# Swapped weights in the attention products, transposes after them, and unread operations behind the last store

## The chip, the cores and the metric

One core of a Trainium2 chip runs the program. TensorE (PE) multiplies matrices, VectorE (DVE) and ScalarE (ACT) work elementwise, GpSimd (POOL) prepares masks, SyncE (SP) issues most DMAs. Each engine executes its own instructions in order, and engines wait for each other by semaphores. The metric is the device time of one execution in microseconds (us); lower is better.

## The reference

Attention over 8 batches x 8 heads x 576 positions x 64, whose first four heads see a causal window of 32 positions and whose last four see every fourth position of a window of 128; then a feed-forward network of width 2048 on the 4608 x 512 result.

```python
scores = scale * np.matmul(q, k.transpose(0, 1, 3, 2))
mask_plain = (rel >= 0) & (rel < window)
mask_dil = (rel >= 0) & (rel < window * dilation) & (rel % dilation == 0)
scores = np.where(masks[None, :, :, :], scores, -1000000000.0)
attn = np.exp(scores - np.max(scores, axis=-1, keepdims=True))
attn = attn / (np.sum(attn, axis=-1, keepdims=True) + 1e-09)
out = np.matmul(attn, v)
# heads side by side, then
h = x @ w_in
g = 0.5 * h * (1.0 + erf(h * inv_sqrt2))
return g @ w_out
```

## The kernel before

The 4608 positions are worked on in nine chunks of 512. Chunk 0 to 7 are the first 512 positions of each batch, chunk 8 holds the last 64 of all batches. Within a chunk the heads go in four pairs, p0 and p1 plain, p2 and p3 with every fourth position. Chunk 8's p2 and p3 are called wide: their windows have 96 keys, the others' 64.

The feed-forward network splits every fp32 number into a rounded part and a rest, so that each product is three matmuls of 128 x 128 weights and 512 columns. For each chunk `ffn_h` makes h in 16 blocks f of 12 matmuls (line 537), `ffn_gelu` applies the gelu on ScalarE and splits the result into g on ScalarE and VectorE, and `ffn_o` makes the output in 16 x 12 matmuls (line 560). A unit below is 12 of these matmuls, so a chunk has 32 units. The order in a chunk is: eight blocks of h, their o, the other eight blocks of h, their o; in the last part the four output blocks d finish one after the other, at units 26, 28, 30 and 32, each with a copy (line 98 or 100) and a store.

The attention of chunk c + 1 is laid into the network of chunk c. `add(c, at, rank, gen)` puts a step at a unit of that chunk, and the steps are emitted as soon as the loop has passed their unit; among equal units a lower rank goes first. Scores (line 296) stand at units 2 and 4, the exponentials from 8.5, the normalisation and `turn` (which lays keys onto partitions by 32 x 32 transposes on VectorE, lines 418 and 423) from 10.5. `av` multiplies attention weights and v: p0 and p1 at unit 24.75, p2 and p3 at 26.75; `xout` then copies the result from PSUM to x on ScalarE (line 98) and subtracts to get the rest on VectorE (line 524). The network's next chunk reads x from unit 32 on. Chunks 0 and 1 are laid out differently, by an order written out by hand, and are not touched by the change.

PSUM is one tile `ps` of eight banks. Banks 0 to 3 hold o, and the scores in between; banks 4 and 5 hold h, and banks 4 to 7 the results of `av`. A quarter of the columns of all four banks belongs to each pair.

In `av` (line 493) v is the weights: 64 keys on the rows, the 64 columns of one head's v. The turned attention weights of 32 queries stream, so a product writes 64 partitions (the head's dimensions) x 32 columns (queries). A pair has 32 such products, which the profile records as 64, since an fp32 product is two. The result has the dimensions on partitions, as the network needs it.

Buffers come from pools: `wpool` (tag "w") holds the network's weights and, by turns, loaded q, k and v; `work` (tag "sm", 7 buffers) holds softmax tiles and turned weights; `xg` holds x, g and scratch.

Of the kernel before, what the change touches and what calls it, by code (L numbers as in the profile page):

```python
# [7 lines left out]
F32 = mybir.dt.float32  # L8
F32R = mybir.dt.float32r
BF16 = mybir.dt.bfloat16  # L10
U32 = mybir.dt.uint32
U16 = mybir.dt.uint16
AF = mybir.ActivationFunctionType
ALU = mybir.AluOpType
AX = mybir.AxisListType

B, H, S, D = 8, 8, 576, 64
WIN, DIL = 32, 4
DM, DFF = H * D, 2048
P = 128  # L20
N = 512
# [6 lines left out]
KB, NU = 32, 4  # L28
# [39 lines left out]
def at_once(gen):  # L68

    e = next(gen)  # L70
    try:
        while True:
            e = gen.send(e[0])
    except StopIteration:
        pass
# [3 lines left out]
def attn_ffn(ctx: ExitStack, tc: tile.TileContext, qk, qk_lp, qk_ld, v, v_ld, w, outT):  # L79
    nc = tc.nc  # L80
    const = ctx.enter_context(tc.tile_pool(name="const", bufs=1))
    wpool = ctx.enter_context(tc.tile_pool(name="wpool", bufs=NF + NW_SPARE))
    xg = ctx.enter_context(tc.tile_pool(name="xg", bufs=12))
    work = ctx.enter_context(tc.tile_pool(name="work", bufs=2))
# [3 lines left out]
    ps = psum.tile([P, 8, 512], F32, name="ps")  # L88
# [179 lines left out]
    def slot(s, u):  # L268
        return u if s.plain or s.rest or s.c < 2 else (u - 1) % NU
# [202 lines left out]
                            to = to[:, (2 * r + a) * KB:(2 * r + a + 1) * KB]  # L472
                        nc.tensor.matmul(to, s.v[rows, a, r, h * D:(h + 1) * D], t, start=True, stop=True)  # L473

    def av(s, px, u0=0):

        yield "p"
        s.px = px
        if s.wide:
            for u in range(u0, u0 + 2):  # L480
                for m in range(3):
                    for r in range(4):
                        rows = slice(32 * r, 32 * r + 32)
                        for h in range(2):
                            nc.tensor.matmul(px(r)[h * D:(h + 1) * D, u * KB:(u + 1) * KB], s.v[rows, u, m, h * D:(h + 1) * D],  # L485
                                             s.t[h][rows, 3 * u + m], start=m == 0, stop=m == 2)
            return
        for u in range(NU):
            for j in range(2):
                for r in (j, 2 + j):  # L490
                    rows = slice(r // 2 * 64, r // 2 * 64 + 64)
                    for h in range(2):
                        nc.tensor.matmul(px(r)[h * D:(h + 1) * D, u * KB:(u + 1) * KB], s.v[rows, u, j, h * D:(h + 1) * D],  # L493
                                         s.t[rows, h * NU + slot(s, u), j], start=True, stop=True)

    def px_four(p, bank):

        return (lambda r: ps[:, bank + r, p * P:(p + 1) * P]), ps[:, bank:bank + 4, p * P:(p + 1) * P]

    def xout(s, px):  # L500
        e = yield "ad" if s.c < 2 else "a"
        s.x = xg.tile([P, 2, N], F32R, tag="xg", name="x")
        if s.wide:
            put = []
            for b in range(2):
                src = px[:, :, b * 64:(b + 1) * 64].rearrange("p r (g i) -> p r g i", g=4)
                dst = [s.x[:, t].rearrange("p (r b i g) -> p r b g i", r=4, b=2, g=4)[:, :, b] for t in range(2)]
                put.append((src, dst))
        elif s.c < 2:

            px = ps[:, s.bank + 1] if s.wide_v else ps[:, s.bank:s.bank + 2, s.p % 2 * 256:s.p % 2 * 256 + 256]
            to = [s.x[:, t] if s.wide_v else s.x[:, t].rearrange("p (k n) -> p k n", k=2) for t in range(2)]
            if s.wide_v and s.plain:
                px = px.rearrange("p (b d i) -> p b d i", d=DIL, i=8)
                to = [y.rearrange("p (d b i) -> p b d i", d=DIL, i=8) for y in to]
            put = [(px, to)]
        else:
            put = [(px, [s.x[:, t].rearrange("p (r i) -> p r i" if s.plain or s.rest else "p (i r) -> p r i", r=4)
                         for t in range(2)])]
        for y, (h, l) in put:  # L520
            copy(e, h, y)
        yield "d"
        for y, (h, l) in put:
            nc.vector.tensor_sub(l, y, h)  # L524
# [44 lines left out]
    def store(c, d, parts=1):  # L569
        for i in range(parts):  # L570
            n = N // parts
            cols = slice(i * n, (i + 1) * n)
            e = yield "ad" if i % 2 == 0 else "d"
            o = work.tile([P, N], F32, tag="go", name="o_sb", bufs=3)
            copy(e, o[:, cols], ps[:, d, cols])
            yield "q"
            (nc.scalar if parts > 1 and e == "a" else nc.sync).dma_start(
                outT[d * P:(d + 1) * P, c * N + i * n:c * N + (i + 1) * n], o[:, cols])
# [5 lines left out]
    jobs = {}  # L584
# [9 lines left out]
    for f in range(NF):  # L594
# [4 lines left out]
        for i, cols in enumerate(parts(f)):  # L599
            k = f"{f}.{i}" if f < HALVED else f"{f}"  # L600
# [7 lines left out]
    for c in range(3):  # L608
        for p in range(NPAIR):
            s, k = xs[c][p], f"{c}.{p}"  # L610
            jobs["qk" + k] = load(s)
            if c == 2:
                continue
            if p % 2 == 0:
                jobs["v" + k] = load_v(s)
            if c == 0:
                jobs["scores" + k] = scores(s, (4, 0, 2, 6)[p])
                jobs["av" + k] = av_wide(s)
                for i in range(2):
                    jobs[f"half{k}.{i}"] = turn_half(s, i)  # L620
            elif p % 2 == 0:
                jobs["scores" + k] = one("p", [scores(xs[c][p + i], 6) for i in range(2)])
                jobs["av" + k] = one("p", [av_early(xs[c][p + i]) for i in range(2)])
            if c == 0 or p % 2 == 0:
                jobs["low" + k] = lowest_two(s, xs[c][p + 1]) if c else lowest(s)
                jobs["sums" + k] = inverse(s)
            jobs["exp" + k] = softmax(s)
            if s.subtract:
                jobs["sub" + k] = subtract(s)
                jobs["sum" + k] = sum_up(s)  # L630
            jobs["norm" + k] = norm(s)
            jobs["turn" + k] = turn_pe(s)
            jobs["x" + k] = xout(s, None)
    for d in range(NC):
        jobs[f"store0.{d}"] = store(0, d)

# [1 line left out]
    for i in range(BURN):  # L638
        rows = slice(32 * (i % 4), 32 * (i % 4) + 32)
        nc.tensor.matmul(ps[rows, 7, 0:2 * KB], ones[rows, 0:KB], ones[rows], start=True, stop=True)  # L640
    begun, ended, wants = set(), set(), {}
    for token in SCHEDULE.split():
        name, _, times = token.partition("*")
        name, _, e = name.partition(":")
        times = int(times or 1)
        if name == "fill":
            bank = 7
# [22 lines left out]
    def add(c, at, rank, gen):  # L670
        steps.append((2 * NF * c + at, rank, len(steps), gen))
# [5 lines left out]
                at_once(f)  # L677
        return gen()

    A_SC, A_E, A_N, A_X, A_QK, A_V = (2, 4), 8.5, 10.5, (24.75, 26.75), 26.5, 3  # L680
    for n in range(2, NCH):
        c = n - 1
        s = xs[n]
        late = n == LAST
        for p in range(NPAIR):
            wide = late and p >= 2
            bank = 4 + 2 * (p - 2) if wide else p // 2 * 2
            if c > 1:
                add(c, (3.25 + .25 * (p % 2)) if wide else A_QK - 32 + .25 * p, 0, load(s[p]))
            add(c, A_SC[p // 2] if not wide else 8.25, 1, scores(s[p], bank))  # L690
            add(c, A_SC[p // 2] + .5 + p % 2 if not wide else 8.5 + (p - 2), 2, lowest(s[p]))
            add(c, A_E + p + (.5 if wide else 0), 3, softmax(s[p]))
            add(c, A_N + p * 1.5 + (.5 if wide else 0), 4, inverse(s[p]))
            add(c, A_N + p * 1.5 + (.5 if wide else 0), 4, norm(s[p]))
            add(c, A_N + p * 1.5 + (.5 if wide else 0), 5, turn(s[p]))
            px = px_four(p, 4)
            at = A_X[p // 2] + (1.75 * (p - 2) if wide else 0)
            for u in (range(0, NU, 2) if wide else [0]):
                add(c, at + .75 * u, 6, av(s[p], px[0], u))
            add(c, at + (1.75 if wide else .25 + p % 2 / 2), 7, xout(s[p], px[1]))  # L700
        add(c, A_V, 0, load_v(s[0]))
        if late:
            add(c, 9, 0, load_v_wide(s[2]))
            add(c, 9.25, 0, load_v_wide(s[3]))
        else:
            add(c, A_V + .25, 0, load_v(s[2]))
    steps.sort(key=lambda t: t[:3])
    at = 0
# [8 lines left out]
    for c in range(1, NCH):  # L717
        gs = {}
        base = 2 * NF * c
        for f in range(half):  # L720
            at_once(ffn_h(c, f, gs))
            upto(base + f + 1)
        for f in range(half):
            for d in range(NC):
                ffn_o(d, f, gs)
                upto(base + half + f + (d + 1) / 4)
        for f in range(half, NF):
            at_once(ffn_h(c, f, gs))
            upto(base + half + f + 1)
        for d in range(NC):  # L730
            for f in range(half, NF):
                ffn_o(d, f, gs)
                upto(base + 3 * half + 2 * d + (f - half + 1) / 4)
            at_once(store(c, d, 2 if c == LAST and d == NC - 1 else 1))


# [99 lines left out]
```

## Time and profile before

| | us |
|---|---|
| median of two runs | 886.18 (885.46 to 886.9) |
| the profiled execution | 885.41 |
| its span | 883.6 |
| PE busy | 871.6 |
| DVE busy | 352.1 |
| ACT busy | 380.6 |
| POOL busy | 9.5 |

The span runs from the first instruction of the profile to the end of the last, transfers included; the execution's own time holds a little around it. A row of a group reads: line, engine, operation, what is written and read with shapes, count, then busy time in us, mean duration of one in ns, and the idle time of the engine ahead of it with what ended it. A row of the timeline reads: start, length in us, engine, line, operation, count. Matmuls overlap in these records, so the time that a block of them takes is read from its start to the start of the next block. PEld is the loading of weights, which runs beside the matmuls.

### The profile page before, as it was taken

To read this page: it belongs to the slowest core of one execution; us is meant where nothing else is said; L and a number is where in the kernel's file an instruction comes from. 1 tells how busy PE (TensorE), PEld (TensorE's weight loads), DVE (VectorE), ACT (ScalarE), POOL (GpSimd) and SP (SyncE) were. 2 spreads that over 40 slices of the span, in tenths; PEclk is the share of its full clock that TensorE was granted. 3 is DMA by queue.
4 is the path that set the end of the run, shared out by engine and by line. 5 is a ranking of instruction groups with operands and counts; after the bars stand their busy time and mean duration, and the time that the engine had idled before them with its cause. 6 is when DMAs were issued, how large, how long until landed. Compare 5 with 4: busy or idle time off the path is not lost.

```text
span 883.6 us, 18852 instructions
## 1 busy us (share of the span) xinstructions
PE 871.6 (99%) x8304; PEld 719.4 (81%) x8304; DVE 352.1 (40%) x597; ACT 380.6 (43%) x1016; POOL 9.5 (1%) x46
## 2 busy tenths in 40 slices
PE   7999999999999999999999999999999999999998
PEld 5888888888888888888888888888888888878886
DVE  8899934621462126321552146213622163212020
ACT  7798535442363227232544235423733272314040
POOL 1000020000000000000000000000000000000000
PEclk9999999999999999999999999999999999999999
DMA  9997431003300330024000510033002410010001
GB/s 363 416 420 281 143 101 46 1 1 134 107 0 1 121 120 1 1 92 148 3 1 1 172 69 0 1 133 108 1 1 85 167 73 1 13 38 1 0 1 48
DMA packets 16930, 75.39 MB, mean 85 GB/s; under 512 B 1872, under 2 KB 2128, under 8 KB 12496
## 3 DMA queue, kind: packets, MB, share of 16 engines
q1 hardware_dynamic: 16704, 74.06, 22.5%
q8 instruction: 65, 1.06, 0.5%
q14 instruction: 17, 0.14, 0.1%
q10 hardware_dynamic: 144, 0.13, 0.0%
HBM read 64.75 MB, written 9.44 MB: 84 GB/s over the span
## 4 chain that ended last, share of the span: by engine, by line
PE 97%; DMA 2%; SPq 0%; issue 0%; DVE 0%; ACT 0%; ACTq 0%; DVEq 0%
PE ps L560 45%; PE ps L537 45%; PE ps L493 3%; PE ps L296 3%; DMA raw_w<-w 2%; PE ps L485 1%; PE ps L473 0%; PE ps L431 0%; PE ps L454 0%; SPq L245 0%; PE ps L282 0%; ACT zeroed L98 0%; SPq L166 0%; DVE spare L190 0%; DVE sm L405 0%
## 5 line engine op out<-in xcount | busy, mean ns | idle before, releaser
L560 PE MATMUL ps<-g,weight 128*128 128x512 f32 x1728 | 401.7, 390 | 0.0
L537 PE MATMUL ps<-x,weight 128*128 128x512 f32 x1728 | 401.3, 390 | 0.0
L537 PEld LDWEIGHTS ps<-x,weight 128*128 128x128 f32 x1728 | 322.9, 188 | 67.9
L560 PEld LDWEIGHTS ps<-g,weight 128*128 128x128 f32 x1728 | 322.9, 188 | 67.2
L549 DVE TENSOR_TENSOR g<-gf,g 128x512 fp32r<-128x512 f32 x144 | 99.7, 693 | 382.6 <-ACT g L98 382.5
L544 ACT ACTIVATE gf<-ps 128x512 f32<-128x512 f32 x144 | 86.1, 598 | 311.1 <-PE ps L537 311.1
L98 ACT CAST g<-gf 128x512 fp32r<-128x512 f32 x143 | 88.8, 621 | 4.5
L380 ACT ACTIVATE sm<-sm,st 128x64 f32<-128x64 f32 (+1 forms) x224 | 74.9, 337 | 0.1
L98 ACT COPY o_sb<-ps 128x512 f32<-128x512 f32 (+1 forms) x34 | 19.7, 582 | 108.4 <-PE ps L560 103.8
L524 DVE TENSOR_TENSOR x<-ps,x 128x512 fp32r<-128x512 f32 (+1 forms) x38 | 30.2, 805 | 86.8 <-ACT x L98 86.8
L98 ACT CAST x<-ps 128x512 fp32r<-128x512 f32 (+1 forms) x37 | 27.0, 749 | 58.9 <-PE ps L493 40.6
L423 DVE STREAM_TRANSPOSE turned<-sm 32x256 f32<-32x256 f32 x104 | 45.4, 436 | 2.0
L380 ACT ACTIVATION_READ_ACCUMULATOR sm<-sm,st 128x1 f32 x224 | 42.1, 188 | 0.0
L296 PEld LDWEIGHTS ps<-raw_qk 64*32 64x32 f32 x2304 | 26.0, 110 | 9.3 <-issue 5.4
L296 PE MATMUL ps<-raw_qk 64*32 64x64 f32 (+1 forms) x2304 | 30.2, 236 | 2.5 <-DMA raw_qk<-qk 2.4
L493 PEld LDWEIGHTS ps<-turned,v_sb 64*64 64x64 f32 x1664 | 25.4, 135 | 4.6 <-issue 4.6
L493 PE MATMUL ps<-turned,v_sb 64*64 64x32 f32 x1664 | 26.9, 220 | 0.0
L405 DVE TENSOR_TENSOR sm<-sm,st 128x512 f32<-128x512 f32 x30 | 20.6, 690 | 0.9
L209 DVE SCALAR_TENSOR_TENSOR weight<-raw_w,spare 128x1024 fp32r<-128x1024 uint32 (+1 forms) x17 | 19.8, 1162 | 0.4
L197 DVE SCALAR_TENSOR_TENSOR raw_w<-raw_w,spare 128x1024 uint32<-128x1024 uint32 (+1 forms) x17 | 19.6, 1155 | 0.0
L418 DVE STREAM_TRANSPOSE turned<-sm 128x512 f32<-128x512 f32 x26 | 18.5, 711 | 0.9
L338 DVE TENSOR_REDUCE st<-sm 128x8 f32<-128x512 f32 x26 | 17.8, 686 | 0.9
(77 smaller groups left out, 252.0 us busy)
## 6 DMA issues: line engine op xcount, KB each, us to landing
v_sb<-v SPq DMA_DIRECT2D x17, 1024.0 KB, 5.2
raw_qk<-qk SPq DMA_DIRECT2D x32, 512.0 KB, 6.8
raw_w<-w SPq DMA_DIRECT2D x15, 1024.0 KB, 17.6
outT<-o_sb SPq DMA_DIRECT2D x35, 256.0 KB, 2.1
mid_w<-w SPq DMA_DIRECT2D x8, 1023.5 KB, 17.6
raw_qk<-qk_ld SPq DMA_DIRECT2D x2, 1024.0 KB, 6.6
v_wide<-v_ld SPq DMA_DIRECT2D x2, 768.0 KB, 6.1
raw_qk<-qk_lp SPq DMA_DIRECT2D x2, 640.0 KB, 5.3
```

The lines of the kernel that those rows point to most:

```text
L98: nc.scalar.copy(out, in_)
L209: nc.vector.scalar_tensor_tensor(weight(f)[:, 1, cols], low, 2.0 ** (-36 if f in TWICE or f in MIDDLE else -43), t.bitcast(F32), op0=ALU.m ...
L296: nc.tensor.matmul(s.sc[32 * r:32 * r + 32, h, c0:c0 + s.nk], x[:, q0:q0 + 32], x[:, k0:k0 + s.nk], start=s.c > 1, stop=s.c > 1 or u == NU ...
L380: nc.scalar.activation(t, s.sc[:, i // NU, at:at + 2 * KB] if s.c < 2 else t, AF.Exp, bias=s.st[:, 0, i:i + 1], scale=SCALE if s.c < 2 els ...
L405: nc.vector.tensor_mul(s.all, s.all, t.unsqueeze(2).broadcast_to((P, 2 * NU, 2 * KB)))
L423: nc.vector.transpose(s.t[32 * to:32 * to + 32, :, r % 2], s.all[32 * r:32 * r + 32, :, j * KB:(j + 1) * KB])
L493: nc.tensor.matmul(px(r)[h * D:(h + 1) * D, u * KB:(u + 1) * KB], s.v[rows, u, j, h * D:(h + 1) * D], s.t[rows, h * NU + slot(s, u), j], s ...
L524: nc.vector.tensor_sub(l, y, h)
L537: nc.tensor.matmul(bank, weights[f][:, t, cc * P:(cc + 1) * P], x[:, xx], start=n == 1 and i == 0, stop=n == parts and i == 2)
L544: nc.scalar.activation(gf, bank, AF.Gelu)
L549: nc.vector.tensor_sub(g[:, 1], gf, g[:, 0])
L560: nc.tensor.matmul(ps[:, d], weights[f][:, t, DM + d * P:DM + (d + 1) * P], gs[f][:, u], start=f == 0 and n == 0, stop=f == NF - 1 and n == 2)
```

## The change

In `av`, for all pairs but the wide ones, weights and streamed operand change places: the turned attention weights are loaded (64 keys x 32 queries) and v streams with its 64 columns. A product now writes 32 partitions (queries) x 64 columns (dimensions). A pair fills two banks instead of four: p0 and p2 banks 4 and 5, p1 and p3 banks 6 and 7. A new step `turn_back` moves the result back to dimensions on partitions by six VectorE transposes out of PSUM, two over 128 partitions and four over 32, into a tile `y` in SBUF; `xout` reads `y` instead of PSUM. In the last chunk the wide pairs' products stand at units 26.25, 27.5, 29 and 30.25 (before: 26.75, 28.25, 28.5 and 30). Behind the last store VectorE and GpSimd get operations whose results nothing reads.

```diff
-        for u in range(NU):
-            for j in range(2):
-                for r in (j, 2 + j):
-                    rows = slice(r // 2 * 64, r // 2 * 64 + 64)
+        bank = 4 + s.p % 2 * 2
+        s.px = ps[:, bank:bank + 2, s.p // 2 * NU * D:(s.p // 2 + 1) * NU * D]
+        for u in range(NU):
+            for j in range(2):
+                for k in range(2):
+                    rows = slice(64 * k, 64 * k + 64)
                     for h in range(2):
-                        nc.tensor.matmul(px(r)[h * D:(h + 1) * D, u * KB:(u + 1) * KB], s.v[rows, u, j, h * D:(h + 1) * D],
-                                         s.t[rows, h * NU + slot(s, u), j], start=True, stop=True)
+                        g = 2 * h + j
+                        nc.tensor.matmul(s.px[32 * g:32 * g + 32, k, u * D:(u + 1) * D], s.t[rows, h * NU + slot(s, u), j],
+                                         s.v[rows, u, j, h * D:(h + 1) * D], start=True, stop=True)
+    def turn_back(s):
+        s.y = work.tile([P, 4, NU, KB], F32, tag="sm", name="y", bufs=7)
+        def part(src, dst, d, j):
+            x = s.px[src].rearrange("p r (u d k) -> p r u d k", d=2, k=KB)[:, :, :, d]
+            y = s.y[dst].rearrange("p (r j) u q -> p r u j q", j=2)[:, :, :, j]
+            nc.vector.transpose(y, x)
+        for d in range(2):
+            yield "d"
+            part(slice(0, P), slice(0, P), d, d)
+        for g in range(4):
+            yield "d"
+            part(slice(32 * g, 32 * g + 32), slice(32 * (g ^ 1), 32 * (g ^ 1) + 32), 1 - g % 2, g % 2)
...
+        A_X = (24.75, 24.75, 26.25, 29) if late else (24.75, 24.75, 26.75, 26.75)
...
+                add(c, at + .25, 7, turn_back(s[p]))
+                add(c, at + .25 + p % 2 / 2, 8, xout(s[p]))
...
+    ta, tb = (wpool.tile([P, 2, 2 * DM], F32, tag="w", name=n) for n in ("of_pool", "of_dve"))
+    rounded = xg.tile([P, 2 * DM], F32R, tag="xg", name="rounded_pool")
+    nc.gpsimd.memset(ta, 1.5)
+    nc.vector.memset(tb, 1.5)
+    def pool_op(k, e):
+        if k == 0:
+            e.tensor_copy(rounded, ta[:, 0])
+        elif k == 1:
+            e.tensor_sub(rounded[:, 0:N], ta[:, 0, 0:N], ta[:, 1, 0:N])
+        elif k == 2:
+            e.tensor_mul(ta[:, 0, 0:N], ta[:, 0, 0:N], ta[:, 1, 0:N])
+        elif k == 3:
+            t = ta.bitcast(U16).rearrange("p k n -> p (k n)")[:, 0:4 * DM].rearrange("p (n t) -> p n t", t=4)
+            e.tensor_copy(t[:, :, 0:2], t[:, :, 1:3])
+        elif k == 4:
+            e.tensor_mul(ta[:, 0, 0:N].rearrange("p (a b) -> p a b", a=8), ta[:, 1, 0:N].rearrange("p (a b) -> p a b", a=8),
+                         tb[:, 0, 0:8].unsqueeze(2).broadcast_to((P, 8, 2 * KB)))
+        elif k == 5:
+            e.tensor_copy(ta[:, 0, 0:N], ta[:, 1, 0:N])
+    for k in range(6):
+        for _ in range(4):
+            pool_op(k, nc.gpsimd)
+    u = tb.bitcast(U32)
+    for _ in range(14):
+        nc.vector.tensor_scalar(u[:, 1], u[:, 1], 3, 0x3FFFF000, op0=ALU.logical_shift_left, op1=ALU.bitwise_and)
+        nc.vector.scalar_tensor_tensor(u[:, 1], u[:, 1], 0xC0000000, u[:, 1], op0=ALU.bitwise_and, op1=ALU.bitwise_or)
+        nc.vector.tensor_sub(tb[:, 1, 0:N], tb[:, 1, 0:N], tb[:, 1, N:])
+        nc.vector.tensor_copy(tb[:, 1, 0:N], tb[:, 1, N:])
```

The order on VectorE in a middle chunk, from the products of p0 and p1 to the first g of the next chunk. Before, with x the four pairs' results and g the network's:

```order
L524 TENSOR_TENSOR x_4776<-ps_72,x_4776 128x512
L524 TENSOR_TENSOR x_4785<-ps_72,x_4785 128x512
L524 TENSOR_TENSOR x_4878<-ps_72,x_4878 128x4x128
L524 TENSOR_TENSOR x_4888<-ps_72,x_4888 128x4x128
L549 TENSOR_TENSOR g_4968<-gf_4966,g_4968 128x512
```

After, where y is the tile of the turned results:

```order
L509 STREAM_TRANSPOSE y_4860<-ps_72 128x2x128 x2
L509 STREAM_TRANSPOSE y_4860<-ps_72 32x2x128 x4
L509 STREAM_TRANSPOSE y_4867<-ps_72 128x2x128 x2
L509 STREAM_TRANSPOSE y_4867<-ps_72 32x2x128 x4
L542 TENSOR_TENSOR x_4874<-y_4860,x_4874 128x512
L542 TENSOR_TENSOR x_4883<-y_4867,x_4883 128x512
L509 STREAM_TRANSPOSE y_4976<-ps_72 128x2x128 x2
L509 STREAM_TRANSPOSE y_4976<-ps_72 32x2x128 x4
L509 STREAM_TRANSPOSE y_4983<-ps_72 128x2x128 x2
L509 STREAM_TRANSPOSE y_4983<-ps_72 32x2x128 x4
L542 TENSOR_TENSOR x_4990<-y_4976,x_4990 128x4x128
L542 TENSOR_TENSOR x_5000<-y_4983,x_5000 128x4x128
```

In front of each two subtractions now stand twelve transposes, six for each pair.

The order on PE in the last chunk, from the products of p0 and p1 to the next chunk's h. Before (L493 are the products of pairs p0 and p1, L485 those of the wide pairs, half a pair in each row; the profile records each of these twice):

```order
L493 MATMUL ps<-turned,v_sb 64x32 x64
L560 MATMUL ps<-g,weight 128x512 x24
L485 MATMUL ps<-turned,v_wide 64x32 x48
L560 MATMUL ps<-g,weight 128x512 x18
L485 MATMUL ps<-turned,v_wide 64x32 x48
L560 MATMUL ps<-g,weight 128x512 x3
L485 MATMUL ps<-turned,v_wide 64x32 x48
L560 MATMUL ps<-g,weight 128x512 x18
L485 MATMUL ps<-turned,v_wide 64x32 x48
L560 MATMUL ps<-g,weight 128x512 x24
L537 MATMUL ps<-x,weight 128x512 x96
```

After (line 497 is the swapped product, 486 the wide one, 578 and 555 the network's):

```order
L497 MATMUL ps<-v_sb,turned 32x64 x64
L578 MATMUL ps<-g,weight 128x512 x18
L486 MATMUL ps<-turned,v_wide 64x32 x48
L578 MATMUL ps<-g,weight 128x512 x15
L486 MATMUL ps<-turned,v_wide 64x32 x48
L578 MATMUL ps<-g,weight 128x512 x18
L486 MATMUL ps<-turned,v_wide 64x32 x48
L578 MATMUL ps<-g,weight 128x512 x15
L486 MATMUL ps<-turned,v_wide 64x32 x48
L578 MATMUL ps<-g,weight 128x512 x21
L555 MATMUL ps<-x,weight 128x512 x96
```

The counts of all products stay, the second and third wide row are farther apart, and 21 instead of 24 of the network's products stand between the last wide row and the next h.

The end of VectorE's queue, after the change, with the semaphores waited for (Activation is ScalarE's, the DMAHW ones belong to transfers), from the last copy of the output to the end of the first of 14 equal rounds; before, the copy was the last row:

```order
L100 COPY o_sb<-ps 128x256 [waits DMAHW4_49,DMAHW5_49,DMAHW3_49,DMAHW6_49,DMAHW1_49,DMAHW7_49,DVE_49,Activation_49]
L763 MEMSET of_dve 128x2048 [waits DMAHW3_49,DMAHW2_49,DMAHW0_49]
L786 TENSOR_SCALAR of_dve<-of_dve 128x1024 [waits DVE_49]
L787 SCALAR_TENSOR_TENSOR of_dve<-of_dve 128x1024 [waits DVE_49]
L788 TENSOR_TENSOR of_dve<-of_dve 128x512 [waits DVE_49]
L789 COPY of_dve<-of_dve 128x512 [waits DVE_49]
```

Everything new stands behind the copy, and each operation waits for one of its own engine.

The end of GpSimd's queue, after the change; before, the selects for the masks were the last to work:

```order
L762 MEMSET of_pool 128x2048 [waits DMAHW2_49,DMAHW1_49,DMAHW3_49,DMAHW0_49,DMAHW5_49,PE_49,DMAHW7_49,Activation_49,Pool_49]
L767 CAST rounded_pool<-of_pool 128x1024 [waits DVE_49,PE_49,Pool_49]
L767 CAST rounded_pool<-of_pool 128x1024 [waits Pool_49] x3
L769 TENSOR_TENSOR rounded_pool<-of_pool 128x512 [waits Pool_49] x4
L771 TENSOR_TENSOR of_pool<-of_pool 128x512 [waits Pool_49] x4
L774 COPY of_pool<-of_pool 128x512x2 [waits Pool_49] x4
L776 TENSOR_TENSOR of_pool<-of_pool,of_dve 128x512 [waits DVE_49,Pool_49]
L776 TENSOR_TENSOR of_pool<-of_pool,of_dve 128x512 [waits Pool_49] x3
L779 COPY of_pool<-of_pool 128x512 [waits Pool_49] x4
```

The memset waits for PE's products of p0 and p1 of the last chunk, whose v lay in that buffer; the first cast for PE's last product that reads the x whose buffer it takes; the first of L776 for VectorE's memset of `of_dve`.

More of the change, by code (lines that the diff above doesn't have):

```diff
@@ L473, in av_early, with av @@
                         nc.tensor.matmul(to, s.v[rows, a, r, h * D:(h + 1) * D], t, start=True, stop=True)
-    def av(s, px, u0=0):
+    def av(s, u0=0):
         yield "p"
-        s.px = px
         if s.wide:
+            s.px = ps[:, 4:8, s.p * P:(s.p + 1) * P]
             for u in range(u0, u0 + 2):
@@ L484, in av, with xout @@
                         for h in range(2):
-                            nc.tensor.matmul(px(r)[h * D:(h + 1) * D, u * KB:(u + 1) * KB], s.v[rows, u, m, h * D:(h + 1) * D],
+                            nc.tensor.matmul(s.px[h * D:(h + 1) * D, r, u * KB:(u + 1) * KB], s.v[rows, u, m, h * D:(h + 1) * D],
                                              s.t[h][rows, 3 * u + m], start=m == 0, stop=m == 2)
             return
+        bank = 4 + s.p % 2 * 2
+        s.px = ps[:, bank:bank + 2, s.p // 2 * NU * D:(s.p // 2 + 1) * NU * D]
         for u in range(NU):
             for j in range(2):
-                for r in (j, 2 + j):
-                    rows = slice(r // 2 * 64, r // 2 * 64 + 64)
+                for k in range(2):
+                    rows = slice(64 * k, 64 * k + 64)
                     for h in range(2):
-                        nc.tensor.matmul(px(r)[h * D:(h + 1) * D, u * KB:(u + 1) * KB], s.v[rows, u, j, h * D:(h + 1) * D],
-                                         s.t[rows, h * NU + slot(s, u), j], start=True, stop=True)
-    def px_four(p, bank):
-        return (lambda r: ps[:, bank + r, p * P:(p + 1) * P]), ps[:, bank:bank + 4, p * P:(p + 1) * P]
-    def xout(s, px):
+                        g = 2 * h + j
[13 more added lines that the diff above has]
+            part(slice(32 * g, 32 * g + 32), slice(32 * (g ^ 1), 32 * (g ^ 1) + 32), 1 - g % 2, g % 2)
+    def xout(s):
         e = yield "ad" if s.c < 2 else "a"
@@ L505, in xout @@
             for b in range(2):
-                src = px[:, :, b * 64:(b + 1) * 64].rearrange("p r (g i) -> p r g i", g=4)
+                src = s.px[:, :, b * 64:(b + 1) * 64].rearrange("p r (g i) -> p r g i", g=4)
                 dst = [s.x[:, t].rearrange("p (r b i g) -> p r b g i", r=4, b=2, g=4)[:, :, b] for t in range(2)]
@@ L517, in xout @@
         else:
-            put = [(px, [s.x[:, t].rearrange("p (r i) -> p r i" if s.plain or s.rest else "p (i r) -> p r i", r=4)
-                         for t in range(2)])]
+            put = [(s.y.rearrange("p r u q -> p r (u q)"),
+                    [s.x[:, t].rearrange("p (r i) -> p r i" if s.plain or s.rest else "p (i r) -> p r i", r=4) for t in range(2)])]
         for y, (h, l) in put:
@@ L632, in attn_ffn @@
             jobs["turn" + k] = turn_pe(s)
-            jobs["x" + k] = xout(s, None)
+            jobs["x" + k] = xout(s)
     for d in range(NC):
@@ L678, in group @@
         return gen()
-    A_SC, A_E, A_N, A_X, A_QK, A_V = (2, 4), 8.5, 10.5, (24.75, 26.75), 26.5, 3
+    A_SC, A_E, A_N, A_QK, A_V = (2, 4), 8.5, 10.5, 26.5, 3
     for n in range(2, NCH):
@@ L695, in attn_ffn @@
             add(c, A_N + p * 1.5 + (.5 if wide else 0), 5, turn(s[p]))
[L696 to L700, printed above, removed]
+            at = A_X[p]
+            add(c, at, 6, av(s[p]))
+            if wide:
+                add(c, at + 1.25, 6, av(s[p], 2))
+                add(c, at + 1.5, 8, xout(s[p]))
+            else:
+                add(c, at + .25, 7, turn_back(s[p]))
+                add(c, at + .25 + p % 2 / 2, 8, xout(s[p]))
         add(c, A_V, 0, load_v(s[0]))
```

## The prediction

> **What bounds the kernel now.** I read the page's busy table, the slices and the chain first, then the groups by line and shape, then the timeline of PE around the products of attention weights and v, and last the timeline of the end.
>
> ```profile
> span 883.6 us, 18852 instructions
> PE 871.6 (99%) x8304; PEld 719.4 (81%) x8304; DVE 352.1 (40%) x597; ACT 380.6 (43%) x1016; POOL 9.5 (1%) x46
> PEclk9999999999999999999999999999999999999999
> PE 97%; DMA 2%; SPq 0%; issue 0%; DVE 0%; ACT 0%; ACTq 0%; DVEq 0%
> ```
>
> TensorE is busy for 99% of the span at the full clock, and 97% of the chain that ends last is its own. So up to the last store the time is the sum of what TensorE executes: a product made shorter shortens the run by just that, and work on VectorE, 40% busy, is free while it delivers in time. Behind the last product that changes, and the change puts work there. The end of the span by its timeline:
>
> ```profile
> 874.79 5.15 PE L560 MATMUL ps<-g,weight 128*128 128x512 f32 x22
> 880.02 0.37 ACT L98 COPY o_sb<-ps 128x256 f32<-128x256 f32 x1 [4.89 <-PE ps L560]
> 880.43 0.42 DVE L100 COPY o_sb<-ps 128x256 f32<-128x256 f32 x1 [20.23 <-ACT o_sb L98]
> ```
>
> VectorE's last copy ends at 880.43 + 0.42 = 880.85. The remaining 2.75 us of the span are the last transfer. The profiled run took 885.41 us, 1.81 more than its span, and 0.77 less than the median of the runs shown, 886.18.
>
> **The change, part by part.**
>
> *1. The products with v swapped (PE).* There are 26 pairs of heads (four in each of six chunks, two in the last) with 64 matmul records each; count, tiles and place in PE's order stay, but each now loads 64 rows x 32 columns as weights and streams 64 columns, where it loaded 64 columns and streamed 32. The rows of the old form, of the scores, which have exactly the new form (64*32, 64x64), and of the nearest others:
>
> ```profile
> L493 PE MATMUL ps<-turned,v_sb 64*64 64x32 f32 x1664 | 26.9, 220 | 0.0
> 195.00 2.07 PE L493 MATMUL ps<-turned,v_sb 64*64 64x32 f32 x128
> 197.00 5.74 PE L560 MATMUL ps<-g,weight 128*128 128x512 f32 x24
> 224.62 1.48 PE L296 MATMUL ps<-raw_qk 64*32 64x64 f32 x128
> 226.03 5.73 PE L537 MATMUL ps<-x,weight 128*128 128x512 f32 x24
> 717.09 1.79 PE L296 MATMUL ps<-raw_qk 64*32 64x96 f32 x128
> 718.80 3.49 PE L560 MATMUL ps<-g,weight 128*128 128x512 f32 x14
> 777.01 1.17 PE L485 MATMUL ps<-turned,v_wide 32*64 32x32 f32 x96
> 778.11 0.96 PE L560 MATMUL ps<-g,weight 128*128 128x512 f32 x3
> ```
>
> From start to start, 128 old products take 197.00 - 195.00 = 2.00 us, 128 of the scores 226.03 - 224.62 = 1.41 us. Two pairs go together, so there are 1664 / 128 = 13 groups, and the gain is 13 x (2.00 - 1.41) = 7.67 us. One thing differs from the scores: they alternate the two halves of the rows from product to product, the new products do so every second time. The products of L485 are ordered in twos like that and take 1.10 / 96 = 11.5 ns each, against 11.0 for the scores and 15.6 for the old ones; at 11.5 the gain is 13 x (2.00 - 1.47) = 6.9 us. The dearest near form, 96 columns streamed, takes 1.71 us per 128: 13 x 0.29 = 3.8 us. I take 7.7, the row of the same form, and keep 3.8 as the other end.
>
> *2. Turning back (DVE).* Each of the 26 pairs gets six transposes out of PSUM: two of 128 x 256 elements, four of 32 x 256.
>
> ```profile
> L423 DVE STREAM_TRANSPOSE turned<-sm 32x256 f32<-32x256 f32 x104 | 45.4, 436 | 2.0
> L418 DVE STREAM_TRANSPOSE turned<-sm 128x512 f32<-128x512 f32 x26 | 18.5, 711 | 0.9
> 204.67 14.58 PE L560 MATMUL ps<-g,weight 128*128 128x512 f32 x63
> 208.12 1.08 DVE L524 TENSOR_TENSOR x<-ps,x 128x512 fp32r<-128x512 f32 x1 [1.13 <-ACT x L98]
> 219.08 0.62 PE L537 MATMUL ps<-x,weight 128*128 128x512 f32 x2
> ```
>
> Time follows the 256 elements of a row, so I take 0.44 us for both kinds: 6 x 0.44 = 2.6 us a pair, 68.6 us in all. None of it is on the path. The second two pairs are the tight case: their products end at 204.67, x is finished at 208.12 + 1.08 = 209.20, and the first product that reads it starts at 219.08, 9.9 us later. Two pairs add 5.3 us of transposes, which leaves 4.6. Nothing else stands in VectorE's queue there, since the last g is finished before these products. ScalarE's copy of x now waits for the transposes, with one store's copy behind it, whose bank the next chunk needs only some us later. Cost 0; without the cover it would be up to 5.3 us in each of six chunks.
>
> *3. The last chunk's order (PE).* The two wide pairs' four groups move by a quarter to half a unit (a unit is 12 FFN products). The last x then has 21 products left before its reader, where it had 24; 21 at 5.74 / 24 are 5.0 us, and the copy and subtraction of such an x take about 2.3. Cost 0.
>
> *4. VectorE's tail.* The memset of 128 x 2048 and 14 rounds of four operations stand behind the last copy on VectorE, so none can begin before it, and each waits for the one before.
>
> ```profile
> L133 DVE MEMSET zeroed<- 128x1024 f32 x1 | 0.9, 912 | 0.2 <-issue 0.2
> L120 DVE MEMSET zeroed<- 128x512 f32 x1 | 0.5, 485 | 0.0
> L190 DVE TENSOR_SCALAR spare<-raw_w 128x1024 uint32<-128x1024 uint32 x15 | 10.3, 690 | 3.7 <-DMA raw_w<-w 3.3
> L197 DVE SCALAR_TENSOR_TENSOR raw_w<-raw_w,spare 128x1024 uint32<-128x1024 uint32 x15 | 18.3, 1217 | 0.0
> L549 DVE TENSOR_TENSOR g<-gf,g 128x512 fp32r<-128x512 f32 x144 | 99.7, 693 | 382.6 <-ACT g L98 382.5
> L100 DVE CAST g<-gf 128x512 fp32r<-128x512 f32 x1 | 0.4, 420 | 0.0
> 136.20 0.68 DVE L332 SCALAR_TENSOR_TENSOR sm<-ps,masks 128x512 f32<-128x512 f32 x1
> 136.92 0.69 DVE L338 TENSOR_REDUCE st<-sm 128x8 f32<-128x512 f32 x1
> ```
>
> The memset: 912 + 2 x (912 - 485) = 1766 ns. A round: 690 + 1217 + 693 + 420 = 3020 ns. An operation that reads its predecessor's result starts 136.92 - 136.20 - 0.68 = 0.04 us behind its end. So the tail is 1.77 + 14 x 3.02 + 57 x 0.035 = 46.1 us; without the gaps, 44.1.
>
> *5. GpSimd's tail.* The memset of its tile waits for late products, so it falls in the last chunk; the first 16 operations wait for the last products that read x, and run beside the last 21.8 us of products, where VectorE is idle. The last 8 (products of 512 elements with a broadcast operand, and copies) need VectorE's memset and run beside the first operations of VectorE's tail. GpSimd's prices, and what happened where both engines worked at once:
>
> ```profile
> L138 POOL COPY masks<-masks 128x64 f32<-128x64 f32 x3 | 0.6, 244 | 0.1
> L143 POOL COPY two_masks<-weight 128x1 f32<-128x1 f32 x1 | 0.2, 190 | 108.7 <-DVE weight L209 108.7
> L104 POOL TENSOR_SCALAR_AFFINE_SELECT two_masks<-two_masks 32x48 f32<-32x48 f32 x24 | 5.4, 235 | 1.3
> 115.17 0.56 POOL L104 TENSOR_SCALAR_AFFINE_SELECT two_masks<-two_masks 32x48 f32<-32x48 f32 x1
> 114.92 0.73 DVE L549 TENSOR_TENSOR g<-gf,g 128x512 fp32r<-128x512 f32 x1 [1.62 <-ACT g L98]
> ```
>
> A copy costs (244 - 190) / 63 = 0.86 ns an element and 0.19 us. Sixteen operations of 512 to 1024 elements come to 14 us by that, 18 if two inputs cost double, so they fit under the last products. The select that began while VectorE was subtracting took 0.56 us instead of 0.235, and the subtraction 0.73 instead of 0.69: the two engines hold each other up, VectorE by 0.04 us, which is what 48 elements cost GpSimd. If that holds for 512 elements, 8 operations cost VectorE 8 x 0.44 = 3.5 us, or 5.3 with two inputs at double price. I take 4.0. The ends: 0.04 for each, 0.3 us; or the whole of the 8 operations, up to 7.5.
>
> The Trainium skill (SBUF — State Buffer, Who interferes with whom) says that a GpSimd operation and a VectorE operation in a two-port mode or with two inputs in SBUF shut each other out for a whole instruction; the stretched select agrees. The skill's GPSIMD Engine Reference, § 3.1, gives 4497 ns for a two-input operation of 2048 elements: an estimate by that page is 1.1 us for 512 elements, and with it the 8 operations would cost VectorE some 6 us and the total would come to 927.5; no row here shows such an operation.
>
> **The sum.** 885.41 - 7.67 + 46.1 + 4.0 - 2.75 (the last transfer, now beside the tail) = 925.1 us on the profiled run's scale; 0.4 of its distance to the median added, 925.5.
>
> **The rivals.**
> - *VectorE is not held up by GpSimd* (0.3 instead of 4.0): 921.8. For it: VectorE lost only 0.04 us in the one overlap seen. Against it: that is all the work of an operation so small.
> - *The swapped products gain little*: from 3.8 us (929.4) down to nothing (933.2). For it: the new order reuses the same rows twice running. Against it: L485 does so too and is quick.
> - *GpSimd ends last.* VectorE ends at about 923 of the span; GpSimd would need over 70 us for its 24 operations from about 850 on, where rows give some 20 to 25. No row shows its two-input or 16-bit operations. From that point on each further us counts whole: some 936 at four times the price (850 + 4 x 21 + 1.8).
> - *The turned products come too late and PE waits at the next chunk's start.* The margin of 4.6 us is used up when a transpose out of PSUM takes 0.44 + 4.6 / 12 = 0.82 us; at 1.0 us PE would wait 12 x 0.18 = 2.2 us in each of six chunks, 938.
> - *Nothing is slower, since operations without a reader are left out of the program.* Then only the gain stays: 877.7, within 2%. It decides as soon as tail and hold-up together come below 903.9 - 885.41 + 7.67 + 2.75 = 28.9 us. Against it: the unread products ahead of the first loads all ran.
>
> ```profile
> L640 PE MATMUL ps<-ones 32*32 32x64 bf16 x54 | 0.9, 236 | 1.0 <-DVE ones L115 1.0
> ```
>
> **How the numbers follow.** My forecast has 0.62; VectorE not held up 0.12, little gain from the products 0.12, GpSimd last 0.08, PE waiting 0.04, nothing run 0.02. The low end is the sum without gaps and without hold-up, 919.4; the high end has the gain at 3.8 and the hold-up at 7.5, 932.5. With half a us for the scatter of the runs the range is 919 to 933; it holds the forecast, the first rival and most of the second. Two per cent, about what a measurement of this kernel can tell from no change, are 903.9; every case but the last is above it: slower 0.98, same 0.02, faster 0.
>
> **What would show it.** The groups of 128 swapped products should stand 1.4 to 1.5 us apart from what follows, PE's last product should end 7 to 8 us earlier, VectorE's transposes should be 156 at 0.44 us with no gap in PE at a chunk's start, and VectorE should run without pause from about 873 to 923. A last product that ends no earlier, rounds of VectorE far from 3.2 us, or GpSimd's records ending after VectorE's would make it wrong.

## The result, and the profile after

The changed kernel takes 925.86 us (median of two runs, 925.75 to 925.97), the kernel before 886.18: 1.045 times as long, 95% interval 1.042 to 1.047. The profiled execution took 925.97 us. Busy times, clock and the chain, from the page after:

```profile
span 924.2 us, 19091 instructions
PE 864.0 (93%) x8304; PEld 710.8 (77%) x8304; DVE 468.2 (51%) x810; ACT 379.9 (41%) x1016; POOL 40.6 (4%) x71
PEclk9999999999999999999999999999999999999955
PE 91%; DVE 6%; DMA 2%; issue 0%; SPq 0%; ACT 0%; ACTq 0%; DVEq 0%
```

PE is busy for 7.6 us less, VectorE for 116 us more, of which 66.7 are the transposes, and it now ends the chain. The low clock in the last two slices falls where PE has no product left. The swapped products and the transposes by shape, then the first two blocks of such products on PE's timeline:

```profile
L497 PE MATMUL ps<-v_sb,turned 64*32 64x64 f32 x1664 | 19.3, 225 | 0.0
L509 DVE STREAM_TRANSPOSE y<-ps 32x256 f32<-32x256 f32 x104 | 46.4, 446 | 1.9
L509 DVE STREAM_TRANSPOSE y<-ps 128x256 f32<-128x256 f32 x52 | 20.3, 429 | 8.8 <-PE ps L497 8.4
```

```profile
195.42 1.48 PE L497 MATMUL ps<-v_sb,turned 64*32 64x64 f32 x128
196.83 5.75 PE L578 MATMUL ps<-g,weight 128*128 128x512 f32 x24
202.51 1.48 PE L497 MATMUL ps<-v_sb,turned 64*32 64x64 f32 x128
203.92 14.59 PE L578 MATMUL ps<-g,weight 128*128 128x512 f32 x63
```

128 records take 196.83 - 195.42 = 1.41 us, to the hundredth what the scores take. The end of PE, by the chain of before and of after:

```profile
858.18 21.77 PE ps L560 x96
```

```profile
850.01 21.77 PE ps L578 x96
```

PE's last product ends at 871.78 instead of 879.95, 8.17 us earlier. Behind it, VectorE's timeline, from the last copy on:

```profile
872.25 0.42 DVE L100 COPY o_sb<-ps 128x256 f32<-128x256 f32 x1 [20.01 <-ACT o_sb L98]
873.05 1.76 DVE L763 MEMSET of_dve<- 128x2048 f32 x1 [0.38 <-issue]
874.85 0.69 DVE L786 TENSOR_SCALAR of_dve<-of_dve 128x1024 uint32<-128x1024 uint32 x1
875.58 1.95 DVE L787 SCALAR_TENSOR_TENSOR of_dve<-of_dve 128x1024 uint32<-128x1024 uint32 x1
877.56 1.41 DVE L788 TENSOR_TENSOR of_dve<-of_dve 128x512 f32<-128x512 f32 x1
879.01 1.15 DVE L789 COPY of_dve<-of_dve 128x512 f32<-128x512 f32 x1
880.19 1.41 DVE L786 TENSOR_SCALAR of_dve<-of_dve 128x1024 uint32<-128x1024 uint32 x1
881.64 1.51 DVE L787 SCALAR_TENSOR_TENSOR of_dve<-of_dve 128x1024 uint32<-128x1024 uint32 x1
883.19 0.98 DVE L788 TENSOR_TENSOR of_dve<-of_dve 128x512 f32<-128x512 f32 x1
884.20 0.72 DVE L789 COPY of_dve<-of_dve 128x512 f32<-128x512 f32 x1
884.95 0.98 DVE L786 TENSOR_SCALAR of_dve<-of_dve 128x1024 uint32<-128x1024 uint32 x1
...
888.42 0.69 DVE L786 TENSOR_SCALAR of_dve<-of_dve 128x1024 uint32<-128x1024 uint32 x1
...
891.59 0.69 DVE L786 TENSOR_SCALAR of_dve<-of_dve 128x1024 uint32<-128x1024 uint32 x1
...
922.88 0.43 DVE L789 COPY of_dve<-of_dve 128x512 f32<-128x512 f32 x1
```

The same stretch on GpSimd, with the length of four operations in the second column:

```profile
848.10 5.05 POOL L767 CAST rounded_pool<-of_pool 128x1024 fp32r<-128x1024 f32 x4 [87.14 <-PE ps L555]
...
864.10 4.37 POOL L774 COPY of_pool<-of_pool 128x1024 uint16<-128x1024 uint16 x4
874.96 6.09 POOL L776 TENSOR_TENSOR of_pool<-of_pool,of_dve 128x512 f32<-128x512 f32 x4 [6.50 <-DVE of_dve L763]
881.12 4.27 POOL L779 COPY of_pool<-of_pool 128x512 f32<-128x512 f32 x4
```

A round of VectorE takes 3.17 us once GpSimd has ended (888.42 to 891.59). The first three take 888.42 - 874.85 = 13.57 us, 4.05 more than three quiet ones, exactly while GpSimd is at its last eight operations. The tail lasts from 872.67 to 923.31, 50.64 us, and 0.89 us of the span follow it, where 2.75 us of transfer followed the last copy before. The ledger on the profiled runs: 885.41 - 8.17 + 50.64 - 1.86 = 926.02, for 925.97 measured.

### The profile page after: what moved, and what is told of

It is laid out like the page before. It is cut to its first block, busy times and chain, and to the rows that moved or that the text cites. A ratio compares the mean times of both kernels' runs of the same rounds, so it can differ in the third digit from the quotient of the medians.

```text
span 924.2 us, 19091 instructions
## 1 busy us (share of the span) xinstructions
PE 864.0 (93%) x8304; PEld 710.8 (77%) x8304; DVE 468.2 (51%) x810; ACT 379.9 (41%) x1016; POOL 40.6 (4%) x71
## 4 chain that ended last, share of the span: by engine, by line
PE 91%; DVE 6%; DMA 2%; issue 0%; SPq 0%; ACT 0%; ACTq 0%; DVEq 0%
PE ps L555 43%; PE ps L578 42%; PE ps L296 3%; DVE of_dve L787 2%; PE ps L497 2%; DMA raw_w<-w 2%; DVE of_dve L786 1%; DVE of_dve L788 1%; DVE of_dve L789 1%; DVE y L509 1%; PE ps L486 0%; PE ps L473 0%; PE ps L431 0%; PE ps L454 0%; DVE of_dve L763 0%
## 5 line engine op out<-in xcount | busy, mean ns | idle before, releaser
L509 DVE STREAM_TRANSPOSE y<-ps 128x256 f32<-128x256 f32 (+1 forms) x156 | 66.7, 440 | 10.7 <-PE ps L497 8.4
L98 ACT CAST x<-y 128x512 fp32r<-128x512 f32 x26 | 22.1, 850 | 73.3 <-DVE y L509 73.3
L542 DVE TENSOR_TENSOR x<-y,x 128x512 fp32r<-128x512 f32 x26 | 22.6, 878 | 0.8
L497 PEld LDWEIGHTS ps<-v_sb,turned 64*32 64x32 f32 x1664 | 17.2, 105 | 4.6 <-issue 2.5
L497 PE MATMUL ps<-v_sb,turned 64*32 64x64 f32 x1664 | 19.3, 225 | 0.0
```

What stands on the lines that cost most here:

```text
L98: nc.scalar.copy(out, in_)
L497: nc.tensor.matmul(s.px[32 * g:32 * g + 32, k, u * D:(u + 1) * D], s.t[rows, h * NU + slot(s, u), j], s.v[rows, u, j, h * D:(h + 1) * D], ...
L509: nc.vector.transpose(y, x)
```

## The experiments

The total fits, but a total can fit by errors that cancel. So the parts were run apart, and then the places where the profile of after did not look as forecast. The results are medians. Each set of runs had one chip, on which the kernel before ran too: its median is 886.71 us beside runs 1 to 4, 885.70 beside runs 5 to 8 and 885.77 beside runs 9 and 10.

**1. The swap alone.** All that stands behind the last store is left out.

```diff
-    ta, tb = (wpool.tile([P, 2, 2 * DM], F32, tag="w", name=n) for n in ("of_pool", "of_dve"))
...
-        nc.vector.tensor_copy(tb[:, 1, 0:N], tb[:, 1, N:])
```

> The changed kernel without the two tails behind the last store. Theory (the swap shortens 13 groups of products by 0.59 us each, the pause of 1.4 us in the last chunk is gone, the transposes are hidden but for 0.2 us): 8 us below the kernel before, about 878 us, ratio 0.991; the last product ends near 872 of the span. Rival (part of PE's earlier end in the changed kernel was chance, only the 7.7 us of the groups are real): 878.5 and the pause back in the trace. Rival (the transposes cost more than they show, the tail's time hid it): 882 or more.

Measured: 877.08 us beside 886.71, ratio 0.990, interval 0.988 to 0.991. The profiled executions, 885.41 and 877.43 us, are 8.0 apart, a little more than the 7.7 us of the products. The medians are 9.6 apart, since the times of the kernel before spread over 2 us (see the end). The transposes cost PE one wait of 0.2 us, in the last chunk.

**2. The tails alone,** on the kernel before (the same lines added to it).

> The kernel before with the two tails alone. Theory (swap and tails add up, nothing of the tail lies beside products): 886.2 + 50.6 of tail - 1.9 of last transfer that it covers = 935 us. Rival (the tail's prices depend on what ran before it): away from 935 by more than 2 us.

Measured: 935.12 us beside 886.71. Swap and tails add up: -9.6 and +48.4 against the kernel before give 925.5 for both, 925.86 was measured; by the profiled executions, -8.0 and +48.9 give 926.3, and 925.97 was measured. Nothing of VectorE's tail hides beside other work.

**3. VectorE's tail without GpSimd's.**

```diff
-    nc.gpsimd.memset(ta, 1.5)
...
-    for k in range(6):
-        for _ in range(4):
-            pool_op(k, nc.gpsimd)
```

> The changed kernel without GpSimd's operations behind the last store. Theory (the first three rounds are long because GpSimd and VectorE hold each other up): all 14 rounds take 3.17 us, and the time falls by 4.0 us to 921.8. Rival (VectorE's first rounds are slow by themselves): the first rounds stay at 5.3 and 4.8 us and the time stays at 925.9.

Measured: 921.73 us, 4.1 below the changed kernel. VectorE's timeline of this run:

```profile
875.25 0.69 DVE L766 TENSOR_SCALAR of_dve<-of_dve 128x1024 uint32<-128x1024 uint32 x1
875.98 1.23 DVE L767 SCALAR_TENSOR_TENSOR of_dve<-of_dve 128x1024 uint32<-128x1024 uint32 x1
877.24 0.69 DVE L768 TENSOR_TENSOR of_dve<-of_dve 128x512 f32<-128x512 f32 x1
877.97 0.43 DVE L769 COPY of_dve<-of_dve 128x512 f32<-128x512 f32 x1
878.42 0.69 DVE L766 TENSOR_SCALAR of_dve<-of_dve 128x1024 uint32<-128x1024 uint32 x1
```

The first round takes 878.42 - 875.25 = 3.17 us, like all others. The long rounds were GpSimd's doing. Set against the lengths here, the rows of the changed kernel show how: from 875.58 on, four operations in a row are each 0.72 us longer, beside GpSimd's four products, and the next four each 0.28 to 0.29 longer, beside its four copies. So each GpSimd operation delayed one VectorE operation, whether that read one operand from SBUF or two and whatever its own length: 4 x 0.72 + 4 x 0.29 are the 4.0 us.

**4. GpSimd's tail without VectorE's rounds** (its memset stays).

```diff
-    for _ in range(14):
-        nc.vector.tensor_scalar(u[:, 1], u[:, 1], 3, 0x3FFFF000, op0=ALU.logical_shift_left, op1=ALU.bitwise_and)
...
```

> The changed kernel without VectorE's 14 rounds, its memset kept. Theory (hold-up both ways): GpSimd's last products take 1.28 us as the ones before them, not 1.46, its last copies 0.7 us by half of the cast's 1024 elements, not 1.02, and the time is about 886. Rival (GpSimd's operations cost 1.46 and 1.02 by themselves): the same rows as in the changed kernel and 888.

Measured: 884.37 us, 1.6 below what was expected, mostly because GpSimd's last eight operations were shorter still. GpSimd's timeline:

```profile
874.73 4.41 POOL L776 TENSOR_TENSOR of_pool<-of_pool,of_dve 128x512 f32<-128x512 f32 x4 [6.50 <-DVE of_dve L763]
879.20 2.64 POOL L779 COPY of_pool<-of_pool 128x512 f32<-128x512 f32 x4
```

The hold-up is mutual: 4.41 + 2.64 us alone, 6.09 + 4.27 beside VectorE's rounds. The size of one term was off: a product with the broadcast operand takes 1.04 us alone (mean 1042 ns of four), less than the 1.28 of a product of two full tiles.

**5. VectorE operations out of PSUM beside GpSimd.** Copies take the place of the 14 rounds.

```diff
+    for i in range(56):
+        nc.vector.tensor_copy(tb[:, 1, 0:N], ps[:, 4 + i % 2])
```

> The changed kernel with 56 VectorE copies of 128 x 512 out of PSUM in place of the 14 rounds, beside the same GpSimd operations. Theory (what holds up is the reading of two inputs, or by two ports, from SBUF, which these copies do not do): each copy keeps 0.69 us and a distance of 0.73, GpSimd's products 1.28 us; 874.85 + 56 x 0.725 + 0.9 + 1.8 = 918 us. Rival (any VectorE operation that writes SBUF is held up by GpSimd): the first ten copies are stretched by together 3 to 4 us, 922.

Measured: 917.83 us. VectorE's timeline, then GpSimd's:

```profile
874.53 31.14 DVE L785 COPY of_dve<-ps 128x512 f32<-128x512 f32 x43
```

```profile
874.65 4.41 POOL L776 TENSOR_TENSOR of_pool<-of_pool,of_dve 128x512 f32<-128x512 f32 x4 [6.50 <-DVE of_dve L763]
879.12 2.64 POOL L779 COPY of_pool<-of_pool 128x512 f32<-128x512 f32 x4
```

A copy every 31.14 / 43 = 0.724 us, the same beside GpSimd as after it, and GpSimd's rows are those of run 4. With one operand read from PSUM, VectorE does not meet GpSimd here, though both write SBUF. That fits the Trainium skill (SBUF — State Buffer, Who interferes with whom), by which the two meet where VectorE uses the port pair it shares with GpSimd; the share that each loses of a stream of operations is only in the runs here, 4.05 us for VectorE and 10.36 - 7.05 = 3.3 us for GpSimd.

**6. The last chunk in the order of before.** PE's last product ended 8.17 us earlier, more than 13 groups give, and a pause of 1.40 us that the profile before has in the third of the wide half pairs was gone. This run puts the wide products back to their old units. The pause on PE's timeline of the kernel before, with the products behind it:

```profile
779.00 1.00 PE L485 MATMUL ps<-turned,v_wide 32*64 32x32 f32 x76
781.41 0.42 PE L485 MATMUL ps<-turned,v_wide 32*64 32x32 f32 x20 [1.40 <-issue]
781.76 4.37 PE L560 MATMUL ps<-g,weight 128*128 128x512 f32 x18
```


```diff
-        A_X = (24.75, 24.75, 26.25, 29) if late else (24.75, 24.75, 26.75, 26.75)
+        A_X = (24.75, 24.75, 26.75, 28.5) if late else (24.75, 24.75, 26.75, 26.75)
...
-                add(c, at + 1.25, 6, av(s[p], 2))
+                add(c, at + 1.5, 6, av(s[p], 2))
...
```

> The swap without tails, with the last chunk's wide products at the units of the kernel before. Theory (the pause of 1.4 us belongs to that order, where two half pairs stand only 3 products apart, and the wait of 0.2 us for the transposes to the new one): the pause is back, the wait is gone, 1.2 us above the swap alone. Rival (the pause is tied to the place in PE's code or to chance): no pause, 0.2 us below the swap alone.

Measured: 879.07 us (878.2 to 881.37), 2.0 above the swap alone. PE's timeline, and a window of it with PE's granted clock in the third column from the right:

```profile
772.03 0.97 PE L486 MATMUL ps<-turned,v_wide 32*64 32x32 f32 x73
774.37 0.65 PE L486 MATMUL ps<-turned,v_wide 32*64 32x32 f32 x23 [1.37 <-issue]
774.95 7.15 PE L578 MATMUL ps<-g,weight 128*128 128x512 f32 x18
```

```profile
776.00:778.00 2.00, 2.00 (x6) 1.61 (x5) 1.15 (x2) 0.16 (x1) 0.00 (x0) 0.50 0.00 0
```

The pause is back, and in this execution it cost twice: the clock stood at half behind it, and 18 products took 7.15 us, where the profile before shows 4.37 for the same 18. The two of the four executions whose mean clock is listed as 1.000 took 878.20 and 878.26 us, the expected 1.2 above the swap alone; the others, at 0.998 and 0.996, took 879.88 and 881.37.

**7. Another order within a pair.** The halves of the rows alternate from product to product.

```diff
-                for k in range(2):
-                    rows = slice(64 * k, 64 * k + 64)
-                    for h in range(2):
+                for h in range(2):
+                    for k in range(2):
+                        rows = slice(64 * k, 64 * k + 64)
```

> The swap without tails, with the products of a pair in another order: the two halves of the rows alternate from product to product, as in the scores. Theory (the form sets the price, the order within does not): groups stay at 1.41 us and the time is that of the swap alone within 0.3 us. Rival (two products in a row on the same rows get in each other's way): groups of 1.3 us or less, 1.4 us below.

Measured: 876.95 us beside 885.70, ratio 0.990, interval 0.988 to 0.991; groups of 1.41 to 1.42 us. The order does not matter.

**8. Every transpose three times.**

```diff
+TIMES = 3
...
-        for d in range(2):
+        for d in (0, 1) * TIMES:
...
-        for g in range(4):
+        for g in (0, 1, 2, 3) * TIMES:
```

> The swap without tails, with every transpose out of PSUM executed three times, so 10.6 us more of VectorE for each two pairs. Theory (the cover of the second two pairs in a middle chunk is 7.4 us, the last chunk has none left, since its wide products already wait 0.2 us for the transposes): PE waits some 1 to 3 us at the start of the next chunk in six chunks and some 10 us in the last, 895 to 907 us. Rival (the transposes are hidden however long): no wait, the time of the swap alone.

Measured: 955.68 us. The expectation was some 50 us too low, and the wait stood elsewhere. PE's waits of this run (in total, times, longest), and its timeline in a middle chunk:

```profile
PE ps L498 <- DVE y L510: 51.7, 12, 7.0
PE ps L487 <- DVE y L510: 10.4, 2, 7.4
```

```profile
204.04 0.86 PE L498 MATMUL ps<-v_sb,turned 64*32 64x64 f32 x64 [1.61 <-DVE y L510]
211.90 1.18 PE L498 MATMUL ps<-v_sb,turned 64*32 64x64 f32 x64 [7.00 <-DVE y L510]
213.02 16.79 PE L579 MATMUL ps<-g,weight 128*128 128x512 f32 x63
```

Not the next chunk's h waits, but the products of p2 and p3, for the transposes of p0 and p1: they write other columns of the same banks, and the program makes them wait until these have been read. 62.1 us are waits. Behind each long one the clock is at half for a while (0.50 from 208 to 216 us in this chunk): here the 63 products that follow take 16.79 us instead of 14.59, and over the six chunks they lose 0.9 to 2.3 us each, 9.6 in all. Most of what is left of the 78.6 us above the swap alone lies in the other products behind these waits, at the same clock.

**9. The second two pairs earlier,** to find how much cover there is.

```diff
-        A_X = (24.75, 24.75, 26.25, 29) if late else (24.75, 24.75, 26.75, 26.75)
+        A_X = (24.75, 24.75, 26.25, 29) if late else (24.75, 24.75, 26, 26)
```

> The swap without tails, with the products of the second two pairs in a middle chunk at unit 26 instead of 26.75, so 9 network products (2.0 us) earlier. Theory (these products write the banks from which the first two pairs' transposes read, and wait for those, with 0.9 us to spare at 26.75): PE waits about 1.1 us ahead of them in each of six chunks, 877.1 + 7 = 884 us, more where a wait lowers the clock. Rival (the tight place is the next chunk's reading of x, as the prediction had it, and that only gains by an earlier start): 877.1.

Measured: 880.62 us, 3.5 above the swap alone, half of what the theory gave. PE's timeline in a middle chunk:

```profile
200.44 0.86 PE L497 MATMUL ps<-v_sb,turned 64*32 64x64 f32 x64
201.63 0.86 PE L497 MATMUL ps<-v_sb,turned 64*32 64x64 f32 x64 [0.34 <-DVE y L509]
202.42 3.92 PE L578 MATMUL ps<-g,weight 128*128 128x512 f32 x16
```

Only p3 waits, since p2's banks are those of p0, whose transposes are done first. Both pairs take 202.42 - 200.44 = 1.98 us instead of 1.41, six times 0.57 us. How much cover the changed kernel has is read from VectorE's timeline of it, in the chunk whose second block of products starts at 202.51:

```profile
196.31 5.30 DVE L509 STREAM_TRANSPOSE y<-ps 128x256 f32<-128x256 f32 x12 [0.85 <-PE ps L497]
```

The twelve transposes end at 201.61, and p3 begins in the middle of the block, at 203.2: the cover is 1.6 us.

**10. Two near half pairs at another place.** Where the pause of run 6 comes from, the profile does not say; it waits for nothing shown. Here the second and third half pair are again 3 network products apart, but both begin 6 network products earlier in PE's program.

```diff
-        A_X = (24.75, 24.75, 26.25, 29) if late else (24.75, 24.75, 26.75, 26.75)
+        A_X = (24.75, 24.75, 26.25, 28) if late else (24.75, 24.75, 26.75, 26.75)
...
-                add(c, at + 1.25, 6, av(s[p], 2))
+                add(c, at + 1.5, 6, av(s[p], 2))
...
```

> The swap without tails, with the last chunk's second and third half pairs again 3 network products apart, but all 6 network products nearer to the beginning than in the kernel before. Theory (the pause comes where one more piece of PE's code is needed soon after the last, which the short products of two near half pairs use up too fast; the place is fixed in the code): a pause of about 1.4 us, but after some 79 to 82 of the third half pair's 96 records instead of 73 to 76, and 878.5 us or more. Rival (the third half pair's products wait for something of their own): the pause after the same 73 to 76 records. Rival (chance): no pause, 877.1.

Measured: 879.44 us (878.12 to 880.31). PE's timeline:

```profile
771.23 1.02 PE L486 MATMUL ps<-turned,v_wide 32*64 32x32 f32 x79
773.46 0.52 PE L486 MATMUL ps<-turned,v_wide 32*64 32x32 f32 x17 [1.22 <-issue]
```

Begun 6 products earlier, the half pair pauses after 79 records instead of 73. Counted from the start of the program it is the same place: in both runs the trace holds 7759 of PE's products ahead of the pause. So the place of the pause goes with PE's count of instructions, not with the data of that half pair. The trace also shows what the queue for instructions (q8 on the page of the profile) brings. In the four profiled executions with the pause (the kernel before and runs 2, 6 and 10), a packet of 16 KB ends within 0.4 us of the pause's start, and PE goes on 1.3 to 1.5 us after the packet's end. In the changed kernel and in runs 1, 7 and 9 the last such packet ended 3.3 to 3.7 us before PE came to its 7760th product, and there is no pause. That fits PE waiting for its next piece of code, which in these runs comes early enough when longer products stand ahead. No run moves such a packet by itself, so the cause is argued from this, not shown.

## Why the prediction came out right, and where it did not

**The swapped products: right.** The row of the scores was the right price: 1.41 us for 128, in run 1 and, in the other order, in run 7. The doubt about the same rows twice running was unfounded. The rival that leaves unread operations out is gone too: VectorE has 213 records more than before, the 156 transposes and all 57 operations of its tail.

**PE's end: 8.17 us earlier, 7.67 forecast.** The groups give about 7.5: a whole middle chunk, at 93.62 us by the two chains where it was 94.77, gained 1.15. The rest is step 3, "Cost 0" for the last chunk's order: it took away the pause of 1.40 us and cost 0.2 us of waiting for p1's transposes, and the first swapped products began 0.4 us later than the old ones had. Run 6 shows the pause, which stood in the profile before as "issue" and was not asked for its cause.

**The transposes: their cost was right, the tight place was wrong.** 0.44 us each and no wait in the middle chunks, as forecast. But the step "the second two pairs are the tight case ... which leaves 4.6" looked only for who reads x. The nearest reader of the transposes' end is p3's product, which writes the banks that p1's transposes read, with 1.6 us to spare (runs 8 and 9). The rival "PE waits at the next chunk's start" had the right mechanism at the wrong place: by run 9 its point is not 0.82 us for a transpose but 0.44 + 1.6 / 12 = 0.57.

**VectorE's tail: right.** A round of 3.17 us, 3.16 forecast; memset 1.76 us, 1.77 forecast. Left out was a gap of 0.38 us ahead of the memset.

**The hold-up: 4.05 us, 4.0 forecast,** and runs 3, 4 and 5 show that it is one. The price of the copies was right (0.615 us alone in run 4, 0.63 worked out), that of the products stood at the dear end (1.04 of 0.63 to 1.07), and the sum had VectorE lose 0.44 us to every operation, or twice that to a product, where it lost 0.72 to a product and 0.29 to a copy. That 4.0 was taken between 3.5 and 5.3 and came out is in good part luck. The estimate by the Trainium skill (GPSIMD Engine Reference, § 3.1: 1.1 us for 512 elements of a two-input operation, and with it some 6 us for the hold-up) was near for one product and too high for the hold-up; the measurement decides. The rival without hold-up is out by run 3, the rival in which GpSimd ends last by the rows after: it ended at 885.4, its first sixteen operations having taken 20.4 us beside the last products, where 14 to 18 were forecast.

**The end of the span: 0.9 us off.** The 2.75 us behind the last copy were taken as gone; 0.89 us stay behind VectorE's last operation. With the 0.5 us more of tail and the 0.5 us gained on PE that makes the 0.9 us between 925.1 and the profiled 925.97. The 0.4 us added for the median stood for a scatter of the kernel before that the two runs of the changed kernel, 0.2 us apart, do not have.

## What to carry to other kernels

Work behind the last product counts whole, and its price can be summed from rows of the same form to a few per cent, if what runs beside it on GpSimd is added: where both worked on SBUF here they held each other up, and each GpSimd operation cost VectorE its own length alone less some 0.3 us (0.72 of 1.04, 0.29 of 0.62). Copies out of PSUM did not meet it. For small fp32 products look at the form, not at the flops: here 32 columns as weights and 64 streamed cost 1.41 us per 128 records, and 64 and 32 cost 2.00. When a buffer's reader gets slower, ask who writes that bank next, in other columns too; it may stand nearer than the reader of the result. The swap alone, 877.08 us, is the better kernel, by 1.0% over the kernel before.

## What the runs showed that was not expected

- A pause of 1.1 to 1.4 us in PE's own program, without a wait that the profile names, after 7759 records in runs 6 and 10 and after 7762 in the kernel before and run 2. It stands behind the landing of a packet of instructions, and it vanished with 18 instead of 3 long products between two blocks of short ones.
- In the profiled executions of runs 6 and 10 the granted clock fell to half at the pause, for 6.8 and 3.4 us (in run 6, 18 products in 7.15 us instead of 4.37); in those of the kernel before and of run 2, with the same pause, it did not. The times of these kernels go with the mean clock listed for each execution: of the 27 of the kernel before beside the runs, those at 0.999 or 1.000 took 885.27 to 885.97 us and those at 0.997 or 0.998 took 886.71 to 887.38, while no execution of runs 1, 7 and 9 is below 0.999. That the pause is what lowers the clock in the executions without a kept profile is likely, but only argued.
- GpSimd's product with a broadcast second operand took 1.04 us for 512 elements, one of two full operands 1.28; 1024 16-bit elements in pairs took 1.05, 1024 fp32 elements with a cast 1.21.
